# A transformer block on one core: a table gives some 1,670 of the planner's operations another place in their engine's order, and the fill at the start gets a smaller factor

## The chip, the cores and the metric

One core of a Trainium2 chip runs the whole program. The metric is the device time of one execution in microseconds; the times shown are medians of several runs on a chip.

## What is computed

Three stages in a row, all float32 in and out.

```python
scores = q @ k^T / 8                        # 4 batches, 8 heads, 576 positions, 64 wide
attn   = softmax(scores, block-causal, blocks of 64)
x      = (attn @ v) as 2304 tokens x 512
h      = ((x @ w1) * (x @ w2)) @ w3         # w1, w2: 512 x 1024, w3: 1024 x 1024
y      = h @ w_out                          # 1024 x 512
r      = maximum(y @ w_in, 0)               # 512 x 2048
out    = (r * r) @ w2_out                   # 2048 x 512
```

The expert weights come as 64-bit floats, so every one of them is converted on the chip.

## The kernel before, in words

**Stages.** The sixteen pairs of heads go through attention one after the other (`pair`, `attend`): TensorE makes the scores of a pair in three groups, VectorE takes the row maxima, ScalarE the exponentials, VectorE the reciprocals of the sums; the weights are then split into two 16-bit parts (`p16`), which the DMA transposes (L1074, issued by SP) turn for the second product. The first three pairs are done in 32 bits, with TensorE transposes (L1100) that ScalarE copies out of one PSUM bank (L1106). For later pairs the values are split too (`split_v`), and four SP transfers a pair (L900, tiles `vmix` and `vsh`) copy the parts into two mixed tiles that `attend` (L1149) reads. Beside attention, the first block's weights are loaded by POOL (L371, L525), joined from 64-bit words on ScalarE and VectorE, scaled by powers of two (`norm_scale`, a small TensorE product at L411) and split; w3 and w_out are multiplied into one matrix (L1245, tile `po`). After each batch of four pairs the first block's products run (`ab_products`, `y_products`, L1245), and y goes to DRAM (L1454). From about 380 us on the second block's weights are converted (`convert_pair`; squares on ScalarE at L1809, summed by a tiny product at L1817), and the second block runs as Strassen-like products (L2110, L2284) with sums on VectorE and squares on ScalarE. The last stores are issued by SP (L2372).

**The order.** Nothing in the program runs where it is written. Every step calls `od.op` with its engine (P TensorE, A ScalarE, V VectorE, G POOL, S SP), a cost in us and a key; there are 4,302 such operations, numbered from 0 as they are declared: 1,573 on V, 1,249 on A, 1,093 on P, 247 on G, 137 on S, and 3 without an engine. `emit` (L126) then plays the program once in modelled time: at each step it takes, over all engines, the operation that could start first, the lowest key first among those that are ready, and emits it. The order so found on each engine is the program's order, which the chip's engines keep, each from its own queue. `RANKS` (L86) adds to the keys of a few numbered operations, `SPARES` (L87) to the time after their inputs from which they count as ready.

**The fill.** From the first memset (L651) until the first weight product, `emit` tells `warm_up` (L643) how long TensorE would idle ahead of the next operation, and `warm_up` puts 128-column products of a zero tile there (L648):

```python
    def warm_up(gap):
        n = int((0.8 * gap - 0.2) / warm_cost[0])
        if n > 0:
            warm_cost[0] = 0.062
        for _ in range(n):
            pe.matmul(warm_out()[:, :P], warm(), warm(), start=True, stop=True)
```

`warm_cost[0]` begins at 0.11. The fill products write a bank that nobody reads. There are 100 of them: 45, 40, 9, 1, 2, 1 and 2 in seven gaps.

Of the kernel before, what the change touches and what calls it, by code (L numbers as in the profile page):

```python
# [80 lines left out]
class Order:  # L81

    RING = 64
    RANKS = {19: -1, 620: 8, 1309: -8, 1310: -8}  # L86
    SPARES = {199: 1.0, 846: 0.3, 929: 0.6, 1284: 1.0, 1507: 0.3, 1510: 1.0, 1582: 1.0, 1585: 0.6, 1909: 1.0}  # L87
    WAIT = 0.03
    TAIL = {"P": 0.15, "A": 0.1, "V": 0.085}
    SAME = {"P": 0.0, "A": 0.125, "V": 0.117}  # L90
# [13 lines left out]
    def op(self, eng, cost, fn, r=(), w=(), key=0.0, spare=0.0):  # L104

        n = len(self.ops)
        o = Op(eng, cost, fn, key + self.RANKS.get(n, 0.0), spare + self.SPARES.get(n, 0.0))
        o.same = self.same.get(eng, 0.0)
# [17 lines left out]
    def emit(self):  # L126
        for b in self.bufs:
            if b.pool in self.after:
                for o in b.ops:
                    o.deps.add(self.after[b.pool])  # L130
            if b.before is not None:
                for o in dict.fromkeys(b.ops):
                    o.deps.update(x for x in b.before.ops if x is not o)
        for o in self.ops:
            o.left = len(o.deps)
            for d in o.deps:
                d.users.append(o)
        free, avail, dma, flight = {}, {}, 0.0, []
        held = {}

        def at(o):
            t = o.ready
            for b in o.banks:
                for e, until in held.get(b, {}).items():
                    if e != o.eng and until > t:
                        t = until
            if o.eng == "G" and isinstance(o.cost, tuple) and len(o.cost) > 3:
                t = max(t, room(o))
            return t

        def descriptors(o):
            return o.cost[3] if len(o.cost) > 3 else 9

        def room(o):
            left = sum(n for _, n in flight)
            for end, n in flight:
                if left + descriptors(o) <= self.RING:
                    return 0.0 if left == sum(m for _, m in flight) else last
                left -= n
                last = end  # L160
            return last if flight and left + descriptors(o) <= self.RING and left == 0 else 0.0

        for n, o in enumerate(self.ops):
            o.n = n
            if not o.left:
                avail.setdefault(o.eng, []).append(o)
        count = 0
        while True:
            best = None
            for eng, todo in avail.items():  # L170
                if not todo:
                    continue
                t0 = free.get(eng, 0.0)
                start = max(t0, min(at(o) for o in todo))
                o = min((o for o in todo if at(o) <= start), key=lambda o: (o.key, o.n))
                if best is None or start < best[0]:
                    best = (start, o, eng)
            if best is None:
                break
            start, o, eng = best  # L180
            if eng == "P" and self.idle:
                self.idle(start - free.get(eng, 0.0))
            avail[eng].remove(o)
            count += 1
            if isinstance(o.cost, tuple):
                issue, move, late = o.cost[:3]
                free[eng] = start + issue
                dma = max(dma, start + issue) + move
                o.end = dma + late
                if eng == "G":  # L190
                    flight[:] = [x for x in flight if x[0] > start] + [(o.end, descriptors(o))]
            else:
                free[eng] = start + o.cost
                o.end = free[eng] + self.TAIL.get(eng, 0.0)
            for b in o.banks:
                held.setdefault(b, {})[eng] = o.end + self.WAIT
            o.fn()
            for u in o.users:
                u.left -= 1
                same = u.eng == eng and eng in "PAV"  # L200
                u.ready = max(u.ready, free[eng] + u.same if same else o.end + self.WAIT + u.spare)
                if not u.left:
                    avail.setdefault(u.eng, []).append(u)
        assert count == len(self.ops), (count, len(self.ops))


@with_exitstack
def fused_kernel(ctx: ExitStack, tc: tile.TileContext, qT, kT, vp, va, w12, w3t, wo, wb, out):
# [432 lines left out]
    warm_cost = [0.11]  # L641

    def warm_up(gap):  # L643
        n = int((0.8 * gap - 0.2) / warm_cost[0])
        if n > 0:
            warm_cost[0] = 0.062
        for _ in range(n):
            pe.matmul(warm_out()[:, :P], warm(), warm(), start=True, stop=True)  # L648
# [1950 lines left out]
```

## Time and profile before

| | |
|---|---|
| median of 3 runs | 828.62 us (827.58 to 830.21) |
| the profiled execution | 828.03 us |
| its span, first to last instruction | 826.30 us |
| TensorE, weight loads | busy 98%, 81% of the span |
| VectorE, ScalarE, POOL | busy 84%, 77%, 18% |

The profile's columns count an engine as busy from the start to the modelled end of its instructions; for TensorE these ends overlap, so that a short wait can lie inside busy time. A wait is put down to the instruction whose semaphore came last. A window's row gives, for each engine, the busy us and in brackets the instructions. The sum of a window's idle time is its length less the busy time.

### The profile page before, as it was taken

How to read it: one execution, taken by the hardware profiler on the slowest of the kernel's cores; microseconds unless marked ns; L12 is line 12 of the kernel's file. 1: busy time of each engine (PE TensorE's matmuls, PEld its weight loads, DVE VectorE, ACT ScalarE, POOL GpSimd, SP SyncE). 2: the span in 40 equal slices, each digit the busy share in tenths (PEclk: the TensorE clock that was granted, in tenths of full speed). 3: DMA queues.
4: the chain of work that ended last, by engine and by line, in shares of the span. 5: the costliest groups of instructions: out<-in, count | busy, mean ns of one | idle time of the engine just before them, and what ended most of it. 6: DMA issues, size and time to landing. Idle time of an engine off the chain costs nothing. (4 is left out here: it accounts for less than half of the span.)

```text
span 826.3 us, 19386 instructions
## 1 busy us (share of the span) xinstructions
PE 809.8 (98%) x7422; PEld 673.0 (81%) x7422; DVE 691.0 (84%) x1637; ACT 639.3 (77%) x1454; POOL 151.4 (18%) x257
## 2 busy tenths in 40 slices
PE   7999999999999999999999999999999999999998
PEld 6456767789779897799878877788888888888887
DVE  6999889988898897837897899999978788686675
ACT  6999979967897787847999978998848646774662
POOL 5021120112111011012324212221221021101010
PEclk9999999999999999999999999999999999999999
DMA  8865767799999899764878664452351132112112
GB/s 339 324 214 183 168 177 156 177 166 226 211 189 185 161 189 200 126 135 156 297 262 302 233 219 148 128 115 46 71 141 16 19 71 59 20 15 65 14 20 58
DMA packets 121885, 123.95 MB, mean 150 GB/s; under 512 B 90560, under 2 KB 99840, under 8 KB 120384
## 3 DMA queue, kind: packets, MB, share of 16 engines
q0 software_dynamic: 27600, 92.39, 38.1%
q1 hardware_dynamic: 94192, 30.32, 22.0%
q8 instruction: 58, 0.95, 0.5%
q14 instruction: 35, 0.29, 0.1%
HBM read 71.17 MB, written 17.83 MB: 108 GB/s over the span
## 5 line engine op out<-in xcount | busy, mean ns | idle before, releaser
L1245 PEld LDWEIGHTS <-w 128*128 128x128 f16 x1536 | 147.1, 98 | 40.4 <-issue 2.8
L2284 PEld LDWEIGHTS <-gs 128*128 128x128 f16 x1104 | 107.8, 98 | 13.4 <-DVE gs L322 0.2
L1245 PE MATMUL ab<-x0h,w 128*128 128x320 f16 x512 | 109.3, 299 | 1.4 <-DVE a L1407 1.4
L1245 PE MATMUL y<-g,w3o 128*128 128x320 f32 (+1 forms) x768 | 109.2, 299 | 0.2 <-DVE a L1407 0.2
L1013 ACT ACTIVATE pf<-s,nm 128x192 f32<-128x192 f32 (+4 forms) x160 | 83.2, 532 | 33.8 <-DVE nm L996 27.9
L1245 PEld LDWEIGHTS y<-g,w3o 128*128 128x128 f32 x768 | 103.3, 188 | 1.9 <-issue 0.7
L1245 PE MATMUL ab<-x1h,w 128*128 128x256 f16 x512 | 88.1, 273 | 0.0
L2110 PEld LDWEIGHTS <-wb 128*128 128x128 f16 x768 | 75.0, 98 | 10.3 <-DVE c L2142 0.5
L2284 PE MATMUL p<-ts,gs 128*128 128x256 f16 x648 | 81.8, 273 | 0.0
L2173 ACT ACTIVATE c<-c,beta 128x512 f32<-128x512 f32 x64 | 45.4, 713 | 41.8 <-DVE c L2142 41.7
L1245 PE MATMUL ab<-x0l,w 128*128 128x320 f16 x256 | 76.5, 299 | 0.0
L1064 DVE SCALAR_TENSOR_TENSOR p<-pf,r,p 128x192 f16<-128x192 f32 (+4 forms) x130 | 67.4, 546 | 4.5 <-ACT p L1057 3.9
L1245 PE MATMUL ab<-x1l,w 128*128 128x256 f16 x256 | 69.8, 272 | 0.0
L1057 ACT ACTIVATE p<-pf,r 128x192 f16<-128x192 f32 (+4 forms) x130 | 67.0, 568 | 2.6 <-DVE r L1030 1.2
L2110 PEld LDWEIGHTS <-st 128*128 128x128 f16 x576 | 56.4, 98 | 7.5 <-issue 0.4
L2284 PE MATMUL p<-wb,gs 128*128 128x256 f16 x456 | 60.5, 273 | 0.0
L2184 DVE TENSOR_TENSOR c<-c,c 128x256 f32<-128x256 f32 x32 | 13.5, 422 | 37.0 <-ACT c L2176 36.9
L320 ACT ACTIVATE gs<-c 128x512 f16<-128x512 f32 x64 | 33.1, 518 | 14.2 <-DVE c L2184 13.9
L988 DVE TENSOR_REDUCE nm<-s 128x2 f32<-128x384 f32 (+1 forms) x64 | 42.2, 686 | 1.1
L379 ACT ACTIVATE raw<-raw 128x512 f32<-128x512 f32 (+1 forms) x53 | 38.6, 729 | 3.7 <-DMA raw<-in_wb 3.7
L288 ACT ACTIVATE g<-a 128x320 fp32r<-128x320 f32 (+1 forms) x64 | 28.3, 442 | 15.5 <-DVE a L1407 14.8
L2176 ACT ACTIVATE c<-c 128x512 f32<-128x512 f32 x64 | 39.5, 621 | 0.8
(294 smaller groups left out, 2026.6 us busy)
## 6 DMA issues: line engine op xcount, KB each, us to landing
raw<-in_wb POOLq DMA_DIRECT2D x32, 512.0 KB, 6.5
raw<-in_w3t POOLq DMA_DIRECT2D x8, 1024.0 KB, 10.0
raw<-in_w POOLq DMA_DIRECT2D x16, 512.0 KB, 4.8
xdram<-cw POOLq DMA_DIRECT2D x16, 512.0 KB, 6.0
yraw<-ydram POOLq DMA_DIRECT2D x12, 512.0 KB, 4.7
vraw<-in_vp POOLq DMA_DIRECT2D x16, 320.0 KB, 4.9
kraw<-in_kT POOLq DMA_DIRECT2D x16, 288.0 KB, 5.9
qraw<-in_qT POOLq DMA_DIRECT2D x15, 288.0 KB, 5.1
```

Source lines behind the costliest of these rows:

```text
L288: od.op(ACT, c_act(n), lambda: act.activation(hi(), src(), AF.Copy), [ks], kh, key)
L320: od.op(ACT, c_act(n), lambda: act.activation(hi(), src(), AF.Copy), ks, kh, key)
L379: act.activation(up, up, AF.Prelu, scale=2.0**-112, alpha=2.0**32)
L988: lambda k=k, t=t, nm=nm, banks=banks: dve.tensor_reduce(out=nm()[:, k], in_=banks[0]()[:, :, S_COL[t] : S_COL[t] + n_keys(t)], op=ALU.max ...
L1013: act.activation(o, view(a, t), AF.Exp, bias=nm()[:, k, a : a + 1], scale=SCALE, accum_out=ssum()[:, k, a : a + 1],)
L1057: lambda o=o, nk=nk, a=a, k=k, w=weights, p16=p16, r=r: act.activation(p16()[:, o : o + nk], w(a, k), AF.Copy, scale=r()[:, k, a : a + 1]),
L1064: lambda o=o, nk=nk, a=a, k=k, w=weights, p16=p16, r=r: dve.scalar_tensor_tensor(out=p16()[:, o + nk : o + 2 * nk], in0=w(a, k), scalar=r( ...
L1245: pe.matmul(acc(), l, r, start=k == 0, stop=k == len(mms) - 1)
L2110: pe.matmul(acc()[:, TH * half : TH * half + TH], lhs(a, kc), y[yn]()[:, kc], start=n == 0, stop=n == len(mms) - 1,)
L2173: lambda src=src, k=k: act.activation(src(), src(), AF.Relu, scale=beta()[:, j, k : k + 1]),
L2176: od.op(ACT, c_act(512), lambda src=src: act.activation(src(), src(), AF.Square), [], ks, K_EVICT)
L2284: pe.matmul(acc()[:, TH * u : TH * u + TH], t()[:, o : o + P], r(b), start=first and n == 0 and u == tiles[0], stop=last and n == 2 and u ...
```

## The change

A table `BEHIND` is added. Its key is an operation's number, its value the numbers of those that are to follow it directly on the same engine. `emit` now plays the program twice. The first time (`run()`) it only notes the order that the keys give; `rows` takes the operations named in the table out of it and puts each behind its key, with the followers of the followers; the second time (`run(lines)`) each engine must take its list in that order, and the operations are emitted. So modelled times no longer choose within an engine. `RANKS` loses an entry and gets two, `SPARES` gets three, and the first factor of the fill goes from 0.8 to 0.68 as long as nothing was filled.

The table has 1,043 keys and 1,669 followers: 668 on V, 509 on A, 362 on P, 73 on G, 57 on S. Of the numbers below, 25, 1, 7 and 17 are loads and memsets of POOL at the start (147 loads the values of the fourth pair, 12 the first weights, 139 and 140 the second pair's queries and keys). 195 is a TensorE transpose, 223 the scores of the second pair's first group, 151 the norm product of the values' scale. 622, 624, 625 and 629 are expert products, 483 is a norm product. On SP, 1520 to 1523 are the four copies of pair 11's values, 1567 a transpose of that pair's weights; 1276 to 1279 the copies of pair 8, 1318 and 1323 transposes of it; 1031 and 1029 copies of pair 7, 1351, 1352 and 1354 of pair 9. 2490 and 2492 are the squares that two L1817 products wait for; 4289, 4291 and 4299 are last stores.

```diff
+    BEHIND = {
+        195: (223, 151), 217: (42, 210), 43: (213,), 44: (215,), 45: (235,), 95: (96,), 305: (335,), 331: (461,),
+        119: (109, 344), 349: (425, 351), 122: (438,), 426: (405,), 826: (440, 431), 622: (483, 624, 629, 625),
...
+        2460: (2463,), 2456: (2472,), 2471: (2477,), 2476: (2482, 2481), 2490: (2492,), 2486: (2156,),
...
+        4225: (4206,), 4241: (4244,), 4242: (4258,), 4260: (4294,), 4287: (4290,), 25: (147,), 1: (12,), 7: (140,),
+        17: (139,), 34: (142, 86), 59: (143,), 99: (125,), 132: (470,), 476: (146,), 492: (498,), 798: (799, 520),
...
+        856: (805, 804), 859: (889,), 914: (925,), 961: (928,), 982: (960,), 1013: (1030, 1028), 1051: (1029,),
+        1071: (1031,), 1318: (1278, 1277), 1323: (1276, 1279, 1337), 1393: (1351,), 1398: (1354, 1448),
+        1447: (1352,), 1472: (1446,), 1503: (1492, 1487), 1567: (1520, 1522, 1521, 1523), 1775: (1799,),
...
+        2055: (4291, 4289, 4299),
+    }
     RING = 64
-    RANKS = {19: -1, 620: 8, 1309: -8, 1310: -8}
-    SPARES = {199: 1.0, 846: 0.3, 929: 0.6, 1284: 1.0, 1507: 0.3, 1510: 1.0, 1582: 1.0, 1585: 0.6, 1909: 1.0}
+    RANKS = {19: -1, 221: 8, 1309: -8, 1310: -8, 2587: 0.3}
+    SPARES = {173: 1.0, 199: 1.0, 846: 0.3, 929: 0.6, 1284: 1.0, 1507: 0.3, 1510: 1.0, 1582: 1.0, 1585: 0.6, 1614: 0.7, 1909: 1.0, 3869: 0.4}
...
+        self.run(self.rows(self.run()))
+
+    def rows(self, seq):
+
+        moved = {n for run in self.BEHIND.values() for n in run}
+        lines = {}
+        for o in seq:
+            todo = [] if o.n in moved else [o.n]
+            if o.eng not in lines:
+                lines[o.eng] = []
+                todo.insert(0, -1 - "PAVGSN".index(o.eng))
+            while todo:
+                n = todo.pop(0)
+                if n >= 0:
+                    lines[o.eng].append(self.ops[n])
+                todo[:0] = self.BEHIND.get(n, ())
+        return lines
...
+                if lines:
+                    k = head[eng]
+                    todo = [lines[eng][k]] if k < len(lines[eng]) and not lines[eng][k].left else []
...
-                if best is None or start < best[0]:
+                if best is None or start < best[0] or lines and start == best[0] and o.n < best[1].n:
...
-            o.fn()
+            if lines:
+                o.fn()
...
-        n = int((0.8 * gap - 0.2) / warm_cost[0])
+        n = int(((0.68 if warm_cost[0] > 0.1 else 0.8) * gap - 0.2) / warm_cost[0])
```

## Rows read from the trace of the kernel before

**Rows 1.** The page: span, two engines' busy time and the chain by engine

```profile
span 826.3 us, 19386 instructions
PE 809.8 (98%) x7422; PEld 673.0 (81%) x7422; DVE 691.0 (84%) x1637; ACT 639.3 (77%) x1454; POOL 151.4 (18%) x257
...
PE 28%; DVE 1%; issue 0%; DVEq 0%
```

**Rows 2.** Busy us by stretch: PE, PEld, DVE, ACT, POOL; PEclk, DMA share, GB/s

```profile
0.00:10.00 10.00, 8.71 (x101) 7.85 (x101) 3.38 (x9) 3.01 (x9) 6.36 (x17) 1.00 0.77 277
10.00:100.00 90.00, 84.06 (x526) 53.51 (x527) 84.13 (x196) 86.22 (x193) 17.15 (x31) 1.00 0.72 246
100.00:200.00 100.00, 97.89 (x910) 77.84 (x910) 91.34 (x242) 82.34 (x216) 14.95 (x27) 1.00 0.84 173
200.00:400.00 200.00, 199.47 (x2212) 172.40 (x2211) 160.89 (x407) 154.41 (x414) 30.51 (x58) 1.00 0.90 181
400.00:600.00 200.00, 197.38 (x1648) 163.18 (x1647) 184.76 (x432) 178.94 (x378) 52.12 (x84) 1.00 0.58 177
600.00:800.00 200.00, 200.00 (x1832) 178.66 (x1830) 150.99 (x323) 124.95 (x233) 28.60 (x38) 1.00 0.22 44
800.00:827.00 27.00, 22.30 (x204) 19.55 (x201) 15.49 (x32) 9.44 (x18) 1.71 (x2) 1.00 0.20 49
```

**Rows 3.** Timeline of TensorE, first 20 us: start, us, what, idle before

```profile
0.99 4.39 PE L648 MATMUL warm_out<-warm 128*128 128x128 bf16 x45 [0.99 <-DVE warm L651]
5.31 2.05 PE L954 MATMUL s<-kraw,qraw 64*128 64x192 f32 x16
...
11.33 0.68 PE L1100 MATMUL tp<-ident,pf 128*128 128x128 f32 x3 [1.63 <-DVE pf L1039]
...
17.60 0.27 PE L648 MATMUL warm_out<-warm 128*128 128x128 bf16 x2 [1.45 <-DVE vsq L508]
```

**Rows 4.** The fill products alone (L648), by stretch: PE, PEld, clock, DMA

```profile
0.90:4.50 3.60, 3.51 (x34) 3.51 (x35) 1.00 0.62 178
...
7.30:9.80 2.50, 2.40 (x40) 2.23 (x40) 1.00 1.01 395
```

**Rows 5.** The keys' tile, first 12 us: its two loads, issue and landing

```profile
L688 POOL DMA_DIRECT2D kraw<-in_kT x2: 539/624/710, 1.3 to 4.3; - x2
...
DMA to landing us min/median/max: 3.5/4.9/6.2
```

**Rows 6.** Timeline of TensorE from 112 to 447 us: products that waited

```profile
114.25 0.97 PE L1149 MATMUL pv_bank<-pt,v 128*64 128x128 f16 x28 [0.43 <-DVE nh L417]
...
118.77 0.30 PE L1245 MATMUL ab<-x0h,w 128*128 128x320 f16 x1 [0.69 <-DVE a L1407]
...
213.88 0.40 PE L954 MATMUL s<-qk 64*128 64x288 f32 x1 [0.53 <-ACT pf L1013]
...
445.32 0.25 PE L1817 MATMUL nq<-ones,wsq 128*128 128x1 bf16 x4 [0.77 <-ACT wsq L1809]
```

**Rows 7.** Timeline of TensorE: eight score products of one form, twice

```profile
13.01 1.24 PE L954 MATMUL s<-kraw,qraw 64*128 64x288 f32 x8
...
42.98 1.52 PE L954 MATMUL s<-kraw,qraw 64*128 64x288 f32 x8
```

**Rows 8.** SP's issues in pair 11; landing of `vsh`; pair 11's attention on TensorE

```profile
267.30 1.13 SPq L900 DMA_DIRECT2D vmix<-v  x2
268.48 1.29 SPq L900 DMA_DIRECT2D vsh<-v  x2
...
282.38 1.24 SPq L1074 DMA_TRANSPOSE pt<-p  x1
...
DMA to landing us min/median/max: 2.2/5.0/8.8
...
291.91 0.52 PE L1149 MATMUL pv_bank<-pt,v 128*64 128x256 f16 x8
```

More of the change, by code (lines that the diff above doesn't have):

```diff
@@ L133, in emit, with run @@
                     o.deps.update(x for x in b.before.ops if x is not o)
-        for o in self.ops:
-            o.left = len(o.deps)
+        for n, o in enumerate(self.ops):
+            o.n = n
             for d in o.deps:
                 d.users.append(o)
+        self.run(self.rows(self.run()))
[13 more added lines that the diff above has]
+        return lines
+    def run(self, lines=None):
+        for o in self.ops:
+            o.left, o.ready = len(o.deps), 0.0
         free, avail, dma, flight = {}, {}, 0.0, []
@@ L161, in room @@
             return last if flight and left + descriptors(o) <= self.RING and left == 0 else 0.0
-        for n, o in enumerate(self.ops):
-            o.n = n
+        for o in self.ops:
             if not o.left:
                 avail.setdefault(o.eng, []).append(o)
-        count = 0
+        seq = []
+        head = dict.fromkeys(lines or (), 0)
         while True:
@@ L183, in emit @@
             avail[eng].remove(o)
-            count += 1
+            seq.append(o)
+            if lines:
+                head[eng] += 1
             if isinstance(o.cost, tuple):
@@ L196, in emit @@
                 held.setdefault(b, {})[eng] = o.end + self.WAIT
-            o.fn()
+            if lines:
+                o.fn()
             for u in o.users:
@@ L203, in emit @@
                     avail.setdefault(u.eng, []).append(u)
-        assert count == len(self.ops), (count, len(self.ops))
+        assert len(seq) == len(self.ops), (len(seq), len(self.ops))
+        return seq
 @with_exitstack
```

171 rows, old and new, of the table BEHIND are left out of this document.

## The prediction

> **What bounds the kernel now.** I read the page first: TensorE is busy 809.8 of 826.3 us, ScalarE 77%, and the chain that ended last is TensorE work alone as far back as the profile follows it, 28% of the span [rows 1]. So the end is set by TensorE's queue, and an order can only gain what TensorE now waits. The table by stretches says where that is [rows 2]: of 16.5 us idle, 1.3 lie in the first 10 us, 5.9 between 10 and 100, 2.1 from 100 to 200, 0.5 from 200 to 400, 2.6 from 400 to 600, none from 600 to 800, and 4.0 behind the last products. In the second row all three compute engines are nearly full: ScalarE 86.2 of 90 us, VectorE 84.1, TensorE 84.1. There the work that makes operands paces TensorE. From 200 us on TensorE runs almost without a gap.
>
> The start was read alone [rows 3]: 45 fill products, then the first scores at 5.31, fill again, 1.63 us until VectorE has scaled the weights, and at 17.60 a wait of 1.45 us behind the sum of the values' squares. Last I read the single waits [rows 6]: each of 0.4 to 0.8 us, on a small step of VectorE or ScalarE that stands late in its own queue.
>
> **The change, part by part.** The sum goes against the profiled execution, 828.03 us (span 826.30 and 1.73 around it); the median of the runs stands 0.59 above that.
>
> Fill. With the new factor the first gap gives 38 products, at most one fewer or more, where it gave 45: (0.68 g - 0.2)/0.11 for the g of some 6.5 that made 45. That is seven of the eight. The first 34 fills take 3.51 us, 0.10 us each, the spacing of the lower clock level (1.2 GHz), though the column says 1.00; the forty of the second group take 2.40, 0.06 each [rows 4]. The seven removed are of the fast kind: 7 x 0.06 = 0.42 us. The load they wait for is issued at 1.3 and lands 3.5 later, at 4.8 [rows 5]; the first scores start at 5.31 [rows 3], so 0.51 can be had at most. I take 0.4. The clock has risen behind 34 fills, so 38 still cover it; if not, the first scores, 2.05 us [rows 3], would take twice that: a loss of 2.05 is the other bound.
>
> The table. It names 668 operations of VectorE, 509 of ScalarE, 362 of TensorE, 73 of POOL and 57 of SP, nearly all for a place a few positions off (counted against the order before: middle displacement 3 or 4, farthest 33). No operation is added or shortened, so ScalarE and VectorE stay as full as they are; only waits can change.
>
> *10 to 100 us.* Entry 195 puts the product that waits 1.45 us at 17.60 behind transposes and scores that don't need it, so this wait goes; next late are those transposes, whose bank ScalarE must first empty. Entries for ScalarE and VectorE put weight conversions behind scores' work or the reverse. What can be had is bounded by the fullest engine: ScalarE's 3.8 us of idle [rows 2]. The other end is a loss: entry 25 issues a 320 KB load ahead of the first weights; at the 277 GB/s of that stretch [rows 2] all behind it lands 1.2 us later, and ScalarE's first conversions wait for that. I take 1.5, under half of 3.8, because engines this full leave little to fill.
>
> *100 to 200.* TensorE idles 2.1. Entry 622 puts three expert products (624, 629, 625) between product 622 and the attention product that today stands behind it and waits 0.43 at 114.25 [rows 6]; what waits next is that product's bank, later. The entry also brings the norm product 483 there from well ahead. I take 1.0, half. Ends: 2.1 gained; 0.7 lost, one more wait like that at 118.77 [rows 6], if the weights that 483 scales are late for it.
>
> *200 to 400.* 0.5 idle; the one visible wait of 0.53 at 213.88 is on an exponential [rows 6]. I take 0.3; ends 0.5 and a loss that is the rival below.
>
> *400 to 600.* 2.6 idle. The largest, 0.77 at 445.32, is a tiny product that waits for a square on ScalarE [rows 6]; entry 2490 puts the pair's second square right behind the first. I take 1.3, half; ends 2.6 and 0.
>
> *Hidden waits.* The same eight score products take 1.24 us at 13.01 and 1.52 at 42.98 [rows 7]: 0.28 of wait inside busy time. Eight pairs of heads have three such groups each in the first 200 us; if half are as late, 12 x 0.28 = 3.4 us. I take 1.6, half of that; ends 3.4 and 0.
> The Trainium skill (Trainium Kernel Development and Optimization, section Performance Expectations) says that a matmul row's busy time is a bad measure of how near a kernel is to its limit, as matmuls are pipelined. Rows 7 bear that out; by busy time alone this term would be zero and the sum 1.6 smaller.
>
> *600 to the end.* No idle to gain before the last products. The three stores that are put first at the end on SP wait for one another, but the very last store still follows VectorE's last step: nothing.
>
> *POOL and SP.* POOL is not short of time; its moved loads and stores (later query and key loads, later stores of y) land under TensorE's backlog. If that cover is gone a load lands late by one load's time, the 1.2 us above. SP's moves are the rival below.
>
> Sum: 0.4 + 1.5 + 1.0 + 0.3 + 1.3 + 1.6 = 6.1 us, so 821.9 in such an execution, and with the 0.59 a median of **822.5**.
>
> **The rivals.**
> *Nothing moves but the fill* (no change). Places a few positions off exchange one wait for another: on engines at 84 to 86 of 90 us [rows 2], an operation that goes earlier pushes its neighbours later by its own half microsecond, the size of the waits in rows 6. Only 0.4 stays: 828.2. For it: the fullness. Against: the waits from 400 to 600 stand beside ScalarE and VectorE idle of 21 and 15 us. That the table doesn't do what it says is no separate case: the planner stops if not every operation was placed.
>
> *The copies of the values come late* (slower). The table moves the four copies of a pair's values on SP behind the transposes of its weights, in pairs 7, 8, 9 and 11 mostly by five to ten places. In pair 11 they are issued from 267.30 on, and entry 1567 puts them behind the transpose at 282.38, which holds SP until 283.62; the four take 1.13 and 1.29, so the last is issued at 286.0. At the median of 5.0 us it lands at 291.0, and the attention product that reads it starts at 291.91 [rows 8]. That leaves 0.9 us: from a landing time of 5.9 on TensorE stands still there, with every later product queued behind it. At the longest, 8.8, it is 2.9 us; in pairs 7, 8, 9 and 11 that makes 11.6, and 822.5 + 11.6 = 834.1. For it: the DMA engines are 0.90 busy from 200 to 400 [rows 2]. Against: the transposes of that pair then start sooner, and the median landing leaves room.
> The Trainium skill (DMA: Bandwidth & Descriptors, section Issuing engines are not separate DMA queues) says that transfers of all issuing engines run on the same 16 DMA engines and interleave, so a copy issued later finds POOL's loads in its way all the same. The spread of landings, 2.2 to 8.8 us [rows 8], agrees.
>
> *All waits go* (much faster). A planner that sees all engines could empty the whole list: 11.2 us of idle between 10 and 600, the 3.4 hidden and the 0.4 of fill are 15.0, so 813.6. For it: 668 of VectorE's 1,573 operations and 509 of ScalarE's 1,249 get another place. Against: ScalarE and VectorE have only 3.8 and 5.9 us free before 100.
>
> **How the numbers follow.** The measurement tells 0.3% from no change, about 2.5 us: faster is below 826.1, slower above 831.1. The forecast (818 to 826) has 0.50, all waits gone 0.15, nothing but fill 0.20, late copies 0.15. Faster is 0.50 + 0.15 = 0.65, the same 0.20, slower 0.15. The range runs from 815, which leaves out half of the third rival, to 830, which leaves out most of the late copies. The forecast's own range is 818 to 826.
>
> **What would show it.** Right: 38 fills or so and the first scores near 4.9; no wait of 1.45 near 17.6; TensorE's idle from 10 to 100 down by one to two, from 400 to 600 near 1.3; ScalarE's and VectorE's busy times as before; the same 200 of 200 us towards the end, begun 6 us earlier. Wrong: an attention product of pairs 7 to 11 that waits for a copy of values, a first score later than 5.3, conversions on ScalarE that wait for loads before 30 us, or idle that only moves from one row of the table by stretches to another. Slow fills right up to the first scores would show the clock bound.

## The result, and the profile after

The changed kernel takes **839.92 us** (median of 4 runs, 838.99 to 841.53) against 829.41 beside it: a ratio of 1.0126, interval 1.0091 to 1.0161. It is slower by 1.3%, where 822.5 was forecast. The profiled execution took 840.67 us, span 838.9, 12.6 more than the one before.

The page (span, busy time, then the chain that ended last by engine), for [rows 1]:

```profile
span 838.9 us, 19389 instructions
...
PE 816.4 (97%) x7430; PEld 674.4 (80%) x7430; DVE 688.9 (82%) x1637; ACT 644.5 (77%) x1454; POOL 150.6 (18%) x257
...
PE 1%; ACT 1%; DVE 0%; issue 0%; ACTq 0%
```

VectorE's and ScalarE's busy times are nearly as before, so no work was added there. But the chain, 28% of the span before, breaks off after 1% on TensorE: near the end it now waits for other engines.

Busy time by stretch, the same columns as [rows 2]:

```profile
0.00:10.00 10.00, 8.90 (x94) 8.04 (x94) 2.92 (x7) 2.51 (x7) 5.83 (x16) 1.00 0.75 243
10.00:100.00 90.00, 85.81 (x547) 54.70 (x544) 82.74 (x200) 87.76 (x198) 17.03 (x30) 0.98 0.71 245
100.00:200.00 100.00, 99.14 (x978) 80.76 (x977) 91.31 (x247) 83.39 (x217) 15.98 (x29) 1.00 0.80 184
200.00:400.00 200.00, 194.08 (x2095) 165.65 (x2090) 151.72 (x390) 147.17 (x394) 27.36 (x53) 0.97 0.80 169
400.00:600.00 200.00, 196.03 (x1625) 160.98 (x1625) 182.28 (x427) 180.20 (x379) 51.43 (x86) 1.00 0.58 182
600.00:800.00 200.00, 197.85 (x1796) 174.01 (x1795) 154.04 (x322) 126.19 (x231) 30.18 (x40) 1.00 0.22 44
```

From 10 to 200 TensorE's idle time fell from 8.0 us to 5.1, more than the forecast's two terms of 1.5 and 1.0. From 200 on it rose in every stretch: 0.5 to 5.9, 2.6 to 4.0, none to 2.2.

A measure that busy time does not blur: every operation of TensorE does the same work in both kernels, so I took its start after less its start before, and of these the median over the 20 us from the time named on, in the time of the kernel before (positive is late; one profile each). All lags further down are this measure.

| us later than before, near | 20 | 100 | 180 | 220 | 480 | 600 | 820 |
|---|---|---|---|---|---|---|---|
| changed kernel | 0.4 | -0.7 | -3.2 | 4.7 | 5.9 | 8.1 | 12.6 |

Three things are added up here: a gain of 4 us by 205, a jump of 8.6 between 205 and 215, and a slow loss of 6.7 from 480 to the end, with 1.2 more between 220 and 480. The jump is one wait. TensorE's timeline at 208 us (start, us, what, idle before):

```profile
208.71 0.52 PE L1360 MATMUL pv_bank<-pt,v 128*64 128x256 f16 x8
215.12 0.53 PE L1360 MATMUL pv_bank<-pt,vsh 128*64 128x256 f16 x4 [5.89 <-DMA vsh<-v]
...
220.76 0.74 PE L1456 MATMUL ab<-x0h,w 128*128 128x320 f16 x2
...
221.47 0.43 PE L1456 MATMUL ab<-x0h,w 128*128 128x320 f16 x2
```

An attention product of pair 7 waits 5.89 us for the copy `vsh`, operation 1031, which the table puts behind a transpose on SP. Behind the wait two equal products take 0.74 us at 220.76 and 0.43 at 221.47. The granted clock says why (windows of the same columns as above):

```profile
205.00:209.20 4.20, 4.20 (x38) 3.46 (x37) 2.87 (x8) 4.02 (x13) 0.94 (x2) 1.00 1.29 175
209.20:215.10 5.90, 0.03 (x2) 0.00 (x0) 0.44 (x1) 0.00 (x0) 0.54 (x1) 0.66 1.01 242
215.10:221.00 5.90, 5.88 (x40) 4.16 (x41) 3.21 (x9) 1.40 (x4) 1.08 (x2) 0.50 0.94 152
221.00:224.00 3.00, 3.00 (x22) 2.13 (x21) 1.71 (x6) 2.73 (x7) 0.00 (x0) 0.94 1.03 259
```

For 6 us after the wait the clock is at 0.50, its lower level of 1.2 GHz. VectorE and ScalarE stand still with TensorE, as the products behind the wait make their operands.

The start, for [rows 3]:

```profile
0.99 4.24 PE L859 MATMUL warm_out<-warm 128*128 128x128 bf16 x38 [0.99 <-DVE warm L862]
5.33 2.52 PE L1165 MATMUL s<-kraw,qraw 64*128 64x192 f32 x16
...
18.91 0.38 PE L859 MATMUL warm_out<-warm 128*128 128x128 bf16 x4 [0.61 <-DVE vsq L719]
```

The 38 fills are there and the wait of 1.45 is down to 0.61, but the first scores are no earlier, and they take 2.52 us where they took 2.05. The prediction's sign for its clock bound is there too: all 38 fills are of the slow kind, right up to the first scores. In the windows below, of the fill products alone, before (first line) and after, thirteen of them run between 4.60 and 5.30 before (0.06 us each) and six after (0.11):

```profile
4.60:5.30 0.70, 0.70 (x13) 0.60 (x11) 1.00 0.95 347
4.60:5.30 0.70, 0.63 (x6) 0.36 (x4) 1.00 0.76 300
```

From 13.20 on the clock is at 0.50 for 3.4 us (the 0.98 in the row of 10 to 100 above, 1.00 before), and eight score products take 2.29 us there, which took 1.24 before [rows 7]:

```profile
13.20:16.60 3.40, 3.38 (x15) 1.97 (x16) 2.07 (x9) 2.46 (x4) 0.73 (x2) 0.50 1.05 424
13.78 2.29 PE L1165 MATMUL s<-kraw,qraw 64*128 64x288 f32 x8
```

The fill products of all gaps together rose from 100 to 108, since the table's order leaves longer gaps behind the first.

### The profile page after: what moved, and what is told of

Same layout as the page of the kernel before. It is cut to its first block, busy times and chain, and to the rows that moved or that the text cites. A ratio compares the mean times of both kernels' runs of the same rounds, so it can differ in the third digit from the quotient of the medians.

```text
span 838.9 us, 19389 instructions
## 1 busy us (share of the span) xinstructions
PE 816.4 (97%) x7430; PEld 674.4 (80%) x7430; DVE 688.9 (82%) x1637; ACT 644.5 (77%) x1454; POOL 150.6 (18%) x257
## 5 line engine op out<-in xcount | busy, mean ns | idle before, releaser
L1456 PE MATMUL ab<-x0h,w 128*128 128x320 f16 x512 | 111.3, 302 | 0.2 <-DVE a L1618 0.2
L1456 PE MATMUL y<-g,w3o 128*128 128x320 f32 (+1 forms) x768 | 111.4, 300 | 0.0
L1224 ACT ACTIVATE pf<-s,nm 128x320 f32<-128x320 f32 (+4 forms) x160 | 83.1, 530 | 23.5 <-DVE nm L1207 22.5
L2495 PE MATMUL p<-ts,gs 128*128 128x256 f16 x648 | 85.0, 273 | 0.5 <-DVE gs L533 0.5
L1275 DVE SCALAR_TENSOR_TENSOR p<-pf,r,p 128x64 f16<-128x64 f32 (+4 forms) x130 | 68.1, 540 | 10.5 <-ACT p L1268 10.1
L1268 ACT ACTIVATE p<-pf,r 128x320 f16<-128x320 f32 (+4 forms) x130 | 68.6, 559 | 7.3 <-DVE r L1241 3.9
L531 ACT ACTIVATE gs<-c 128x512 f16<-128x512 f32 (+1 forms) x64 | 32.9, 516 | 17.7 <-DVE c L2395 17.6
L1199 DVE TENSOR_REDUCE nm<-s 128x2 f32<-128x640 f32 (+3 forms) x64 | 42.3, 681 | 0.6
L1611 ACT ACTIVATE a<-ab,ab_back 128x320 f32<-128x320 f32 (+1 forms) x64 | 31.7, 497 | 12.2 <-PE ab L1456 9.6
L1665 POOL DMA_DIRECT2D ydram<-ys x32 | 18.0, 564 | 128.3 <-ACT ys L1661 123.8
```

What stands on the lines that cost most here:

```text
L531: od.op(ACT, c_act(n), lambda: act.activation(hi(), src(), AF.Copy), ks, kh, key)
L1199: lambda k=k, t=t, nm=nm, banks=banks: dve.tensor_reduce(out=nm()[:, k], in_=banks[0]()[:, :, S_COL[t] : S_COL[t] + n_keys(t)], op=ALU.max ...
L1224: act.activation(o, view(a, t), AF.Exp, bias=nm()[:, k, a : a + 1], scale=SCALE, accum_out=ssum()[:, k, a : a + 1],)
L1268: lambda o=o, nk=nk, a=a, k=k, w=weights, p16=p16, r=r: act.activation(p16()[:, o : o + nk], w(a, k), AF.Copy, scale=r()[:, k, a : a + 1]),
L1275: lambda o=o, nk=nk, a=a, k=k, w=weights, p16=p16, r=r: dve.scalar_tensor_tensor(out=p16()[:, o + nk : o + 2 * nk], in0=w(a, k), scalar=r( ...
L1456: pe.matmul(acc(), l, r, start=k == 0, stop=k == len(mms) - 1)
```

## The experiments

All start from the changed kernel; only its table of moves is cut, and a move that is taken out leaves its operation at the place of the planner's order (the order without the table). Where whole parts go, the diff shows the first and the last entry that does. Ratios are to the kernel before, with their intervals.

### Which part of the table costs

**Pair 7's two copies put back.**

```diff
-        1051: (1029,),
-        1071: (1031,),
```

> The changed kernel without its two entries for pair 7's copies of values on SP (operations 1031 and 1029 stay where the planner had them; all other 1,667 moves stay). Theory: the 5.89 us wait of the attention product at 215.12 and the half clock behind it cost 9 us together, so the time falls from 839.9 to about 831 (829 to 833), the wait is gone, and operations at 220 us run 3 to 4 us earlier than in the kernel before. Rival: behind that wait stands another one (a bank or an exponential of pair 7 that is just as late), so the time stays at 836 to 840 with a new wait in the same stretch.

Measured: 835.61 us, ratio 1.0061 (1.0036 to 1.0086). The same products in its profile:

```profile
209.17 0.33 PE L1359 MATMUL pv_bank<-pt,vsh 128*64 128x256 f16 x4
...
212.21 0.43 PE L1455 MATMUL ab<-x0h,w 128*128 128x320 f16 x2
```

The wait is gone. From the `vsh` product to the fourth such pair of products it takes 3.04 us here, and 5.64 in the changed kernel (215.12 to 220.76): the half clock cost 2.6 us up to there, 8.5 with the wait. In the profile the gain is 7.1 us of the 9 expected; the median gained 4.3 and misses the theory's 829 to 833. Its ten runs lie in two bunches, 831.8 to 834.5 and 836.7 to 838.0, and the profile is one of the lower. The mean granted clock is 0.998 in every run of the lower bunch and 0.994 to 0.996 in the upper one, which so spent more time at half clock; behind what wait is not shown, since the one trace is of the lower bunch.

**The first two thirds of the table (1,004 moves), the late third (661), and no table.** For the first two thirds:

```diff
-        2690: (2669, 2671, 2668),
...
-        2055: (4291, 4289, 4299),
```

For the late third:

```diff
-        195: (223, 151),
...
-        2039: (2058,),
-        2055: (4291, 4289, 4299),
```

For the third kernel the same down from the first entry to the last, so that nothing is left.

> The table for the first two thirds alone: entries for operations with numbers under 2575 (to about 470 us), without pair 7's two; behind that the planner's own order. Theory: the order of the late part costs 7 us by itself, so this one keeps the 3 to 4 us gained by 207 us and loses nothing later: 825.5 (824 to 828). Rival: the late loss is a follow-up of the changed early part (loads that arrive in another order, the clock), not of the late order: then about 831, as the kernel with only pair 7 mended.

> The table for the late part alone: entries for operations from 2575 on (from about 470 us), the planner's own order before that, the new ranks and fill. Theory: 829.4 + 7 = 836.5 (834 to 838), the loss spread over 480 to 830 us in waits of TensorE for VectorE's and ScalarE's small steps. Rival (late loss is a follow-up of the early part): 829, no change.

> The change without any table: the new fill factor, the new ranks and spare times alone. Theory: none of the loss and little of the gain is theirs: 829 (827.5 to 830.5). Rival: the new ranks and spare times carry the 3 to 4 us gained by 207 us, then 825.5; or they carry part of the loss, then over 831.

Measured: the first two thirds 827.82 (0.9975, 0.9948 to 1.0002), the late third 836.14 (1.0078, 1.0050 to 1.0106), no table 829.31 (0.9993, 0.9972 to 1.0015).

Without a table the new ranks, spare times and fill are worth nothing that can be measured: its first scores start at 5.00 instead of 5.31, near what the fill's term said (0.31 of 0.4), in one profile each. The late third costs 6.3 us by itself. In the profiles its lag grows by 6.7 from 480 to the end, by the same steps as in the changed kernel, so the loss isn't handed down from the early part. The first two thirds come out 2 us short of the theory. They lose 3.4 us between 440 and 480, at the seam to the planner's order, where VectorE waits 2.35 us for a store before it may write its tile again; that profile, 830.43, is one of the longest of its ten runs (823.3 to 831.4).

**The early part alone**: moves of operations that ran before 195 us, without pair 7's copies and without the load that entry 25 puts early (420 moves).

```diff
-        769: (774, 775), 1072: (1017,), 1304: (785, 791),
+        769: (774,),
...
-        25: (147,),
...
-        1051: (1029,), 1071: (1031,),
...
-        2055: (4291, 4289, 4299),
```

> The table for operations that ran before 195 us alone, without pair 7's two copies and without the early load of values on POOL (operation 147 behind 25); the planner's order behind that. Theory: the gain of the change lies wholly here, 4 us by 200 us against the kernel before, and the early load costs 1 of it at the start: first scores at 5.0 and not 5.3, and 824.5 (823 to 826). Rival: what is gained early is lost at the seam or later, since the operand work behind is no sooner done: 828 to 830.

Measured: **823.94 us**, ratio 0.9931 (0.9907 to 0.9954), the fastest kernel of the study. Its first scores start at 4.77. Its busy time by stretch, and its chain by engine:

```profile
10.00:100.00 90.00, 85.99 (x553) 55.07 (x555) 83.44 (x199) 88.00 (x196) 16.99 (x31) 1.00 0.72 244
100.00:200.00 100.00, 98.88 (x975) 80.58 (x973) 90.58 (x247) 82.29 (x215) 17.29 (x32) 1.00 0.77 189
200.00:400.00 200.00, 198.43 (x2159) 171.31 (x2158) 161.52 (x404) 154.97 (x414) 30.24 (x58) 1.00 0.91 178
...
600.00:800.00 200.00, 200.00 (x1832) 178.63 (x1830) 150.82 (x321) 127.55 (x238) 27.58 (x36) 1.00 0.22 44
```
```profile
PE 28%; DVE 1%; issue 0%; DVEq 0%
```

Before 200 us it has the changed kernel's 85 to 86 of 90 and 99 of 100, and behind it the full stretches and the long chain on TensorE of the kernel before. The lags of these kernels, and of two that come below or above:

| us later than before, near | 20 | 100 | 180 | 220 | 480 | 600 | 820 |
|---|---|---|---|---|---|---|---|
| no table | -0.3 | -0.3 | -0.2 | -0.2 | 0.3 | 0.3 | 0.5 |
| late third | 1.6 | 1.6 | 1.8 | 2.4 | 3.8 | 6.0 | 10.5 |
| early part | -1.2 | -2.3 | -4.3 | -4.0 | -3.8 | -3.8 | -3.8 |
| pair 7's copies back | 0.5 | -0.5 | -3.1 | -3.1 | -1.1 | 1.1 | 5.5 |
| POOL's moves back (below) | -0.3 | -1.3 | -3.9 | -4.9 | -3.5 | -1.3 | 3.2 |

What a row has at 20 us is in part chance: ten kernels of the study have the planner's order for the first 190 us, as the upper two rows do, and their lags at 20 lie between -0.8 and 3.4. What a row gains or loses behind 20 us repeats: from 20 to 180 the lag falls by 3.1 to 3.7 in all seven kernels with the table's early part, and changes by at most 0.3 in the others.

### Why the copy came late

**The late copies alone**, in the planner's order.

```diff
-        195: (223, 151), 217: (42, 210),
...
         1051: (1029,), 1071: (1031,),
...
-        2055: (4291, 4289, 4299),
```

> The planner's own order with only the two entries for pair 7's copies of values on SP (operation 1029 behind 1051, 1031 behind 1071); fill, ranks and spare times as changed. Theory: the late copy costs by itself. The copy is then issued at about 209.8 instead of 197.2 and lands 7 to 11 us later, at 217 to 221, and the attention product that reads it, due some 212.5 to 213, waits 4 to 8 us and runs at the half clock behind it: 834 to 841, most likely 837. Rival: the wait needs the rest of the table, which makes TensorE come early there: then under 2 us of wait and 829 to 831.

Measured: 829.04 us, ratio 1.0011 (0.9994 to 1.0028). The copy is issued at 208.54, even later than in the changed kernel, and only this is left of the wait (who waited for it, us and times; and issue to landing):

```profile
  PE pv_bank L1181: 1.2, 1
...
DMA to landing us min/median/max: 4.5/4.5/4.5
```

So its place behind the transposes is not enough: the rival's outcome holds. What differs is what else moves then. POOL in the changed kernel, around the copy's issue at 203.91, and the copy's landing:

```profile
202.30 0.54 POOL L920 DMA_DIRECT2D va<-in_va  x1
202.88 0.54 POOL L902 DMA_DIRECT2D vraw<-in_vp  x1
203.50 0.55 POOL L899 DMA_DIRECT2D kraw<-in_kT  x1
204.06 0.54 POOL L896 DMA_DIRECT2D qraw<-in_qT  x1
204.85 0.54 POOL L920 DMA_DIRECT2D va<-in_va  x1 [0.26 <-issue]
```
```profile
DMA to landing us min/median/max: 11.2/11.2/11.2
```

Five loads, 384 + 320 + 288 + 288 + 384 = 1,664 KB, are issued in 3.1 us. In the planner's order a load of values (1421) and two stores (790, 796) stand between the first and the last of them. That load and the second store wait for other engines and so spread the others (by 2.83 and 3.79 us in the kernel below); the table puts all three behind. One of the five, the 320 KB load 1346, comes later than before, where it was issued at 195.29: the table brings the loads together, and four of them forward.

**POOL's moves around pair 7 put back**, the late copies kept.

```diff
-        1422: (1346, 1420), 1424: (790, 1514, 1513), 1515: (1421,), 1426: (1766, 796),
+        1426: (1766,),
```

> The changed kernel without the seven moves of POOL around pair 7 (loads 1346, 1420, 1421, 1513, 1514 and stores 790, 796 back in the planner's order on POOL); pair 7's two copies on SP stay moved, as every other entry. Theory: the copy landed late because POOL's new order issues five loads, 1,664 KB, within 3 us around it (202.3 to 204.9), while the copy and the DMA transposes share the same engines. In the planner's order one load of 384 KB stands there and the rest comes later. So the copy lands within 7 us of its issue, the attention product waits under 2 us, no half clock, and the time is about that of the kernel without the late copies: 832 to 836. Rival: it is the place behind the transposes on SP alone, as forecast: then it still lands 11 us after its issue, the wait stays 5 to 6 us, and the time stays at 838 to 841.

Measured: 832.57 us, ratio 1.0043 (1.0026 to 1.0061), with the copy still behind its transpose, issued at 203.36:

```profile
201.60 0.54 POOL L919 DMA_DIRECT2D va<-in_va  x1
204.98 0.55 POOL L901 DMA_DIRECT2D vraw<-in_vp  x1 [2.83 <-ACT p L1267]
...
210.81 0.54 POOL L895 DMA_DIRECT2D qraw<-in_qT  x1
```
```profile
DMA to landing us min/median/max: 3.6/3.6/3.6
```

3.6 us instead of 11.2, no wait, 7.4 us of the median back. The rival is out: it took both moves, SP's copy made late and POOL's loads brought together. The loads' bytes alone are not the reason: in the kernel with pair 7's copies put back POOL issues the same five loads at the same pace, and they land in 4.7 to 6.3 us, where in the changed kernel four of the five take 9.5 to 10.8. What holds the transfers up when the loads meet the late copy and the transposes was not taken apart. The Trainium skill (DMA: Bandwidth & Descriptors, section Issuing engines are not separate DMA queues) says that transfers of all issuing engines share the same 16 DMA engines; the two landings agree, as the loads of one engine delayed the copy of another.

### The late loss

**One engine's entries at a time.** TensorE's entries of the late third alone (the first that stays below), then all but these (the second). Two of TensorE's and 22 of the others are left out: in the order that they ask for, operations of the engines wait for one another in a circle.

```diff
         2690: (2669, 2671, 2668),
...
```
```diff
         2216: (2618, 2619),
...
```

> The late part of the table (from about 470 us), TensorE's entries alone (226 of 228); the other engines in the planner's order. The kernel with the whole late part was 7 us slower from 470 us to the end. Theory: TensorE's own new order brings products ahead of the additions on VectorE that empty their bank, and that is the loss: 835 to 837. Rival: the loss comes from VectorE's and ScalarE's entries, and TensorE's alone cost nothing: 828.5 to 830.5.

> The late part of the table without TensorE's entries: VectorE's, ScalarE's and POOL's alone (411 of 433). Theory (TensorE's order is the cause): 829 to 831. Rival (VectorE's and ScalarE's order is the cause): 835 to 837. If both halves cost, each by itself lies above 832, and what was made to go together was taken apart.

Measured: 846.05 (1.0198, 1.0160 to 1.0236) and 896.55 (1.0810, 1.0771 to 1.0849). Both are worse than the whole: an order of products with the old order of their operands, or the reverse. The third case of the expectation; it says nothing of the cause, only that such an order can't be taken in halves by engine.

**One stretch's entries at a time.** Those of 470 to 600 us (310 moves), of which these are the first and the last that stay whole:

```diff
         2690: (2669, 2671, 2668), 2695: (2716, 2701, 2703),
...
         3143: (3186,),
```

> Of the late part of the table only the entries for operations that ran from 470 to 600 us before. Theory: each stretch loses by its own entries; the kernel with the whole late part lost 2.6 us from 480 to 600 us and 4.5 behind that, so this one loses the 2.6 and then runs level: 832 (831 to 833). Rival: the loss is one of the whole chain to the end (what comes late once stays late and adds up), then it goes on behind 600 us: 834 to 836; or the loss belongs to the later entries, then 829.

Measured: 833.09 us (1.0040, 1.0008 to 1.0071). Its lag grows from 2.7 at 500 to 5.2 at 600 and is 5.3 at the end. Each stretch loses by its own entries; the other 4.5 us of the late third belong to those behind 600. No run took those apart. In the kernel with the late third TensorE waits 2.2 us there in six single waits, all for VectorE, which is busy 155 of the 200 us from 600 on, so a full engine is not what these waits show.

The two halves of that stretch, one profile each; of the first, the first and last entry, of the second, the first and last that stay whole:

```diff
         2690: (2669, 2671, 2668), 2695: (2716, 2701, 2703),
...
         2970: (2755,),
```
```diff
         2811: (2825, 2813), 2830: (2870,),
...
         3143: (3186,),
```

> Of the late part only the entries for operations that ran from 470 to 510 us (95). Theory A: VectorE's pause of 1.4 us at 483 comes from these and makes it late for the full stretch behind, so TensorE loses 2 to 2.5 us between 500 and 600 us by them alone. Theory B: the stretch behind loses by its own entries: TensorE's lag from 500 to 600 us changes by under 0.5 here, though the pause at 483 is there.

> Of the late part only the entries for operations that ran from 510 to 600 us (215). Theory A (VectorE comes late from before): without the pause at 483, TensorE's lag from 500 to 600 us changes by under 0.7. Theory B (the stretch's own entries): it grows by 2 to 2.5, in the same small waits of products for VectorE.

Measured: the first half's lag stays at -0.3 from 500 to the end; the second half's grows from -0.4 to 3.0. So theory B: the pause at 483 us is harmless, the entries from 510 on are the loss. This is that stretch without a table, and in the kernel with the late third (columns of the windows above):

```profile
512.00:600.00 88.00, 87.33 (x760) 73.51 (x759) 87.61 (x192) 77.17 (x148) 19.16 (x26) 1.00 0.41 93
```
```profile
512.00:600.00 88.00, 86.40 (x727) 70.08 (x725) 85.00 (x184) 74.76 (x145) 18.56 (x26) 1.00 0.40 96
```

Without the table both TensorE (87.33 of 88) and VectorE (87.61) are full. With it both have gaps: TensorE's single waits from 500 to 610 are for VectorE (1.3 us in five, 0.5 in two without the table). VectorE's one single wait is for ScalarE (0.7 us, 0.5 without), so its other gaps have no releaser named.

**One operand put back.** In the kernel with the entries of 470 to 600, a product at 528.04 waits for a half of `g` that VectorE makes too late:

```diff
-        2821: (2832,), 2823: (2819, 2833, 2926, 2861),
+        2823: (2926, 2861),
-        2822: (2834, 2927, 2875),
+        2822: (2927, 2875),
```

VectorE's timeline ahead of that, in the kernel with the entries of 470 to 600: two conversions of weights (L1819) and their scaling (L2108) stand before the half of `g`.

```profile
525.50 0.42 DVE L1819 TENSOR_TENSOR sf<-sf 128x256 f32<-128x256 f32 x1
...
526.44 0.42 DVE L1819 TENSOR_TENSOR sf<-sf 128x256 f32<-128x256 f32 x1
526.77 0.48 DVE L2108 SCALAR_TENSOR_TENSOR wb<-sf,sig,wb 128x256 f16<-128x256 f32 x1
...
527.57 0.41 DVE L387 TENSOR_TENSOR g<-r,g 128x256 f16<-128x256 f32 x1
```

> The entries of 470 to 600 us as before, less four: VectorE's split 2834 and ScalarE's 2832, 2819 and 2833 in front of it, which go back to the planner's places (two conversions, 2840 and 2841, stay moved, but now stand behind the split). In the kernel with these four the split ends at 527.98, and TensorE's product 2898, which was due about 0.65 us sooner, waits inside its 1.47 us; TensorE falls 0.9 us further behind there. Theory: that step is this one operand's place: product 2898 takes 0.81 again, and the step between 500 and 540 us shrinks from 1.1 to under 0.4, the other steps up to 600 us staying as they are (1.4 together). Rival: VectorE is full, so what goes ahead of it there makes the next operand late by as much: the step stays at 0.8 to 1.1 in a wait a few products on.

Measured: 831.93 us (1.0019, 0.9994 to 1.0044). First TensorE's wait with the four entries, then without them:

```profile
528.04 1.04 PE L2481 MATMUL o<-wb,g 128*128 128x512 f16 x4 [0.48 <-DVE g L387]
```
```profile
528.28 0.27 PE L2175 MATMUL p<-t4l,wb 128*128 128x256 f16 x1 [0.77 <-DVE t4l L387]
```

The wait moved three products on, to the next half that VectorE makes. The step in the lag is about 1 us by 530 in both. The rival.

**Two conversions put back**, which VectorE does ahead of both halves:

```diff
-        2900: (2843, 2845),
+        2900: (2843,),
-        2855: (2840, 2860, 2841),
+        2855: (2860,),
```

> The entries of 470 to 600 us, less those that move VectorE's two conversions of weights 2840 and 2841 (0.42 us each) ahead of the splits 2834 and 2862, and less ScalarE's 2845, which must stand behind 2841. All other entries, the split 2834's own among them, stay. Theory: VectorE has no free time there, so each operation moved ahead of a due one delays it by its own length, 0.84 us for the two; with them back, products 2898 and 2871 wait under 0.15 us together (0.93 before) and the step between 500 and 540 us falls from 1.1 to under 0.3. Rival: the two conversions are due themselves, and what they wait shows behind 540 us: then TensorE's lag from 500 to 600 us stays at 2.5.

Measured: 834.41 us (1.0047, 1.0019 to 1.0075); the lag grows by 2.7 from 500 to 600, the first product waits 0.1 us, the second still takes 0.28 us longer, and two more, at 532 and 536, now take 0.39 and 0.46 longer. The rival again: the wait goes from one product to the next. That this comes of VectorE's being full is argued from the row above; which set of entries would have to go was not found.

### The rest

**The best of the first 470 us**: the first two thirds, with the early load, pair 7's copies and POOL's seven moves put back as well (996 moves).

```diff
-        25: (147,),
-        1422: (1346, 1420), 1424: (790, 1514, 1513), 1515: (1421,), 1426: (1766, 796),
+        1426: (1766,),
-        1051: (1029,), 1071: (1031,),
```

> The table for operations under 2575 (to about 470 us) with three things put back: pair 7's two copies on SP, POOL's seven moves around pair 7, and the early load 147. Theory: with these out, the order of the first 470 us is worth what the kernel with POOL's moves put back showed in its profile, 4.5 to 5 us by 440 us, and the late part was the only loss left there (6.8 us from 480 us on): 823.5 (822.5 to 825). Rival: at the seam to the planner's order near 470 us it loses the 2 to 3 us that the kernel with the first two thirds of the table lost there: 825.5 to 828.

Measured: 825.05 us (0.9939, 0.9914 to 0.9964). In the profile it is 5.7 us ahead at 220 and 4.8 at 440, as the theory has it, and loses 1.8 at the seam. It can't be told from the early part alone.

**The early load of values**, alone in the planner's order, then added to the early part:

```diff
+        25: (147,),
```

> The planner's own order with one entry alone: the load of values 147 (320 KB) directly behind the first keys on POOL, ahead of the constants. Theory: the keys land later (at a median of 7.0 us after their issue, before 5.0), the first scores start at 5.3 and not at 5.0 and take 2.5 and not 2.05 us, and about 1 us is lost by 20 us: 830.3 (829.5 to 831.5). Rival: the loss of the changed kernel at the start is that of other entries: first scores at 5.0, 829, no change.

> The kernel with the table up to 195 us, with the early load 147 put back and nothing else. Theory: with the table's other moves at the start the load costs, as the keys of the next pair and the first weights are issued behind it: TensorE is 1 to 1.9 us later by 20 us and 825 to 826 in all. Rival: it costs nothing, as in the planner's order, and the differences at the start were chance in the landing of the first keys: 823.5 to 824.5.

Measured: alone 828.65 (0.9980, 0.9957 to 1.0004), no loss, first scores at 5.07; with the early part 825.35 (0.9942, 0.9923 to 0.9961), first scores at 5.12 instead of 4.77 and 0.9 us later at 20 us, but 0.5 ahead of the early part at the end of its profile. The intervals overlap. A loss of about a microsecond at the start is seen, within what chance makes there, and a loss at the end is not shown. The changed kernel's 2.52 us for the first scores is not this load's: it came up with the load in some kernels only (2.10 with POOL's moves back) and without it in others (2.40 with the entries of 470 to 600, 2.68 with the late third less TensorE's entries). All the profiles in which the first scores take over 2.06 us have 38 slow fills ahead of them.

## Why the prediction was wrong

*Fill* (0.4): the gain is there, the premise that 38 fills still cover the rise of the clock failed. In the ten kernels with the planner's early order the first scores start at 4.64 to 5.16, in the one profile of before at 5.31. But in eight of the eighteen profiles with 38 fills, the changed kernel's among them, all 38 are of the slow kind; the first scores take up to 2.92 us there, and 3.4 us at a clock of 0.50 follow in each of the eight between 12 and 23 us (a stretch at 0.50 there in two of the other ten as well). In the changed kernel's profile this cost 0.5 us in the first scores and 1.05 in the eight products at 13.78. That is less than the stated bound of 2.05, which had no place in the sum. The medians show no price: without a table 829.31, before 829.83 beside it.

*10 to 100 and 100 to 200, with the hidden waits* (1.5 + 1.0, and 1.6 in the first 200 us): right in sum. With the fill these are 4.5; the early part alone is 4.3 ahead at 180, 4.1 more than without a table. Visible idle makes up 3.0 of it in the changed kernel; the share of the hidden waits was not measured by itself. The waits of 0.43, 0.69 and 1.45 that the steps named are gone or down to 0.61.

*200 to 400* (0.3): this is where the forecast failed first. The late copies were its rival, at a chance of 0.15 and four times 2.9 us. The mechanism and the engine were right: a copy that lands too late stops TensorE. The room of 5.9 us was that of pair 11; pair 7's copy, issued at 203.91 for a product due at 209.23, had 5.3, and that the wait also came to 5.89 is chance. Three sizes were wrong. One pair was hit, not four: the later pairs' copies landed in 2.2 to 4.8 us, and no product waited for them. The landing took 11.2 us, beyond the 8.8 taken as longest from [rows 8]: those rows show copies amid POOL's old order, and the table changed that order as well. And behind a stop of 5.9 us the clock fell, 2.6 us more, a cost that no step had, although the rows of the start show products at both levels [rows 4]. So 1 x (5.9 + 2.6) = 8.5 stands in place of 11.6.

*POOL and SP*: the sentence that POOL's moved loads and stores land under TensorE's backlog is the one that failed. I priced a load's being late and a copy's being late one by one, and not what loads brought together do to a copy issued among them.

*400 to 600* (1.3) and *600 to the end* (nothing): wrong in sign, together 6.7 us of loss from 480 on. The row of 200 us [rows 2] showed VectorE with 15 us idle and I read room from it. The room lies before 510 us; from 512 to 600 VectorE is busy 87.61 of 88. The rival "nothing moves but the fill" had the mechanism, an operation that goes earlier pushes its neighbours later, but I applied it to the first 100 us, where it did not hold. And for the stretch behind 600, 4.5 of the 6.7 us, the step had no loss end at all: TensorE full there means that there is nothing to gain, and everything to lose. Why its entries lose, with VectorE not full, stays open.

The medians of the parts add up to most of the result: early part -0.7%, copies with POOL's burst +0.8%, late third +0.8%, together 0.9 of the 1.3% measured. What is left lies within the intervals.

## What to carry to other kernels

When a reordering moves transfers on two queues, lay both new issue orders side by side around each tile that is due soon: the price of a late copy depends on what is issued around it, and its landing times in the old order do not bound it. Where a fill is cut, look at the spacing of its last products in several profiles, not in one. Cut the table of stretches fine enough that a full engine shows (88 us here, not 200), and give each stretch in which two engines are full a loss end, even where there is no idle time to gain. A long reordering is best taken by stretch and kept where it pays: here the first 195 us of the table alone made 823.94 of 829, and the rest gave it back.

## What the runs showed of the hardware

The same 128 KB copy, behind the same transpose, landed in 3.6, 4.5 and 11.2 us, depending on what POOL issued around it (384 KB 1.8 us ahead and 320 KB 1.6 us behind; 320 KB just ahead and a store behind; five loads of 1,664 KB in 3.1 us). A stop of TensorE of 5.9 us was followed by 6 us at half clock; the stop of 1.2 us at the same place in the kernel with the late copies alone was not, the clock staying at 1.00. The same 38 fill products, from 0.99 us on, reached the upper clock level before their end in ten profiles and not in eight. I had expected none of the three.
